# Splitting two key loads of a fused attention and feed-forward kernel into rows 0 to 119 and a shared strip of rows 120 to 127

## The chip, the cores and the metric

The kernel runs on one core of a Trainium2 chip. The metric is the device time of one execution in microseconds, as the median of several runs. A profile of one execution of each kernel is at hand: it tells when each engine's instructions ran, what they waited for, and what the DMA queues moved. The engines are called PE (TensorE), DVE (VectorE), ACT (ScalarE), POOL (GpSimd) and SP (SyncE).

## The reference

Attention over 4 batches, 8 heads, 768 positions and a head size of 64, and behind it a feed-forward layer. Heads 0, 2 and 6 are causal over all keys; the others see a window of 64 positions and the first 4 keys.

```python
scores = scale * np.matmul(q, k.transpose(0, 1, 3, 2))
stream_keep = causal & (is_sink | in_win)
mask = np.where(retr[0, :, 0, 0, None, None], full_mask, stream_mask)
scores = np.where(mask[None, :, :, :], scores, -1000000000.0)
...
a = a / (np.sum(a, axis=-1, keepdims=True) + 1e-09)
return np.matmul(a, v).astype(np.float32)
...
x = np.ascontiguousarray(attn_out.transpose(0, 2, 1, 3)).reshape(B * S, H * D)
h = np.maximum(np.maximum(x @ w1, x @ w2), x @ w3)
return (h @ w_out).astype(np.float32)
```

## The kernel before

The order of all work is written out by hand. `PROGRAM` (lines 84 to 150) is a list of short items; each names a step and its engines, and every engine runs its own instructions in the order in which the items issue them. Nothing is rescheduled.

Batch 0 is loaded differently from the others, since nothing can be computed before it arrives. Its 768 positions are taken in two halves of 384 and its eight heads in four pairs, `PAIRS` = (0,2), (1,3), (4,6), (5,7), counted from 0. `load_pairs` (line 198) brings the keys (`ks`) and the queries (`qs`) of one pair and one half into a staging tile of 128 partitions, three positions to a partition, so that each partition of each head is one run of 768 bytes. These partitions are the "rows" of the title. An item `hl 1 2 2 ss` (line 88) means half 1, from pair 2 on, two pairs, keys and queries both issued by SP: four transfers of 128 rows, two heads and 192 numbers, 192 KB each. `cast_pair` (line 216) turns a staged pair into 16-bit numbers (`kn`, `qn`, line 220), and `turn_pair` (line 228) transposes them on PE into the tile `KQ` that the scores use.

The values of batch 0 come as `vs` (line 298; half 1 is one transfer of 768 KB, item `load_v 0 1 s` in line 91). POOL casts them into `vn` (line 500), PE sorts their rows with `every3` into `vb` (line 508), and ACT and DVE copy these to `va` (line 513).

From batch 1 on, keys and queries come through POOL's queue with a cast on the way (`kq`, line 261, items `load`), four heads at a time, and DVE transposes them into `KQ` (line 275, items `turn`). The scores of these batches are at line 677, their exponentials at line 694, masks at line 380, the product with the values at line 720, and the feed-forward layer at lines 440 (three weights, `w0t`, `w1t`, `w2t`), 448 and 452 (their maximum) and 465 (the output).

SP issues its transfers strictly in order, and so an item `gs 0` (line 286) can hold up what stands behind it: it copies two numbers of a weight into the tile `gates`, which can't be issued before that weight has landed. Each transfer issued by SP or ACT raises one of eight counters, in turn, and before a counter is used again the transfer that used it last has to have landed. A transfer more or less therefore changes which earlier transfer each later one waits for.

Of the kernel before, what the change touches and what calls it, by code (L numbers as in the profile page):

```python
# [12 lines left out]
AF = mybir.ActivationFunctionType  # L13
ALU = mybir.AluOpType

GUESS = (1, 0, 1, 0, 0, 0, 1, 0)
PAIRS = ((0, 2), (1, 3), (4, 6), (5, 7))
ROWS = ((0, 7), (1, 4), (2, 5), (3, 6))
# [135 lines left out]
def fast(ctx, tc, keep, q, k, v, is_retrieval, n_sink, window, moe_w1, moe_w2, moe_w3, moe_w_out, w_t, woutt, out):  # L154
# [4 lines left out]
    P = 128  # L159
# [4 lines left out]
    HALF = S // 2  # L164
    HB = HALF // P
# [4 lines left out]
    assert (H, S, D, DMdl) == (8, 768, 64, 512) and 0 < window <= 64 and 0 <= n_sink <= 64  # L170
    near = [h for h in range(H) if not GUESS[h]]

# [23 lines left out]
    staged, cast, KQs, landed = {}, {}, {}, {}  # L196

    def load_pairs(half, hp, n, engines):
        for nm, src, eng in zip(("ks", "qs"), (k, q), engines):
            st = (  # L200
                pairs2.tile([P, 4, HB, D], FP32, tag=nm, name=nm) if n == 2
                else once.tile([P, 2 * n, HB, D], FP32, name=f"{nm}{hp}")
            )
            for h in range(0, 2 * n, 2):
                h0, h1 = PAIRS[hp + h // 2]
                eng.dma_start(
                    out=st[:, h : h + 2],
                    in_=src[0, h0 : h1 + 1 : h1 - h0, half * HALF : (half + 1) * HALF].rearrange(
                        "h (p j) d -> p h j d", p=P
                    ),  # L210
                )
            for i in range(n):
                staged.setdefault((half, hp + i), []).append(st[:, 2 * i : 2 * i + 2])
                landed[half, hp + i] = st[0:1, 2 * i, 0, 0:2]

    def cast_pair(half, hp, engines):
        cast[half, hp] = []
# [65 lines left out]
    def gate(engine, x):  # L283
        dst = gates[:, next(n_gate)]
        if engine is nc.sync:
            engine.dma_start(out=dst, in_=x)
        else:
            engine.tensor_copy(out=dst, in_=x)
# [21 lines left out]
    def load_first(half, hp, n, e="sc"):  # L310
        by = {"s": nc.sync, "c": nc.scalar}
        load_pairs(half, hp, n, [by[x] for x in e])
# [11 lines left out]
    def idle_work(n):  # L324
# [11 lines left out]
        out=kb[:, 2:4], in_=kb[:, 2:4], compare_op=ALU.is_ge, fill=0.0,  # L336
# [3 lines left out]
        out=kb[:, 3], in_=kb[:, 3], compare_op=ALU.is_gt, fill=0.0,  # L340
# [3 lines left out]
        out=kb[:, 1:5:3], in_=kb[:, 1:5:3], compare_op=ALU.is_gt, fill=0.0,  # L344
# [7 lines left out]
        out=every3, in_=every3, compare_op=ALU.not_equal, fill=1.0,  # L352
# [4 lines left out]
    if n_sink > 0:  # L357
# [4 lines left out]
        out=far, in0=kb[:, 0:5], scalar1=FAR, scalar2=-FAR, op0=ALU.mult, op1=ALU.add  # L362
# [74 lines left out]
    def hidden(b, half, wi, ni, op=None):  # L437
        yy = psum(b, half)
        for ks in range(KS):
            nc.tensor.matmul(  # L440
                yy[:, 0:HALF],
                w_t[wi][:, ks, ni * P : (ni + 1) * P],
                xT[b, half, ks].rearrange("p a t -> p (a t)"),
                start=(ks == 0), stop=(ks == KS - 1),
            )
        if wi == 0:
            acc[b, half, ni] = accp.tile([P, HALF], FP16, tag="acc", name="acc")
            op(out=acc[b, half, ni], in_=yy[:, 0:HALF])  # L448
            return
        if wi == 2:  # L450
            hT[b, half, ni] = htp.tile([P, HALF], FP16, tag=f"hT{ni}", name=f"hT{ni}")
        nc.vector.tensor_tensor(  # L452
            out=acc[b, half, ni] if wi == 1 else hT[b, half, ni],
            in0=yy[:, 0:HALF], in1=acc[b, half, ni], op=ALU.max,
        )
# [59 lines left out]
    def prep_x(b, half, heads, what, op):  # L515
        by_row = b == 0 and half in sorted_halves
        vs = staged_v[b, half] if not by_row else va[0][:, :, half * HB : (half + 1) * HB, 0:D]
        dst = vx[b % 2]
        hs = slice(*map(int, heads.split(":")))
        which = list(range(*hs.indices(H)))  # L520
        xs_ = slice(near.index(which[0]), near.index(which[-1]) + 1)
        n = len(which)
        assert near[xs_] == which
        if what == "r":
            s0 = 2 * half
            k0 = (1, 0)[half]
            op(out=dst[64:P, xs_, s0 : s0 + 2, 0:D], in_=vs[64:P, hs, k0 : k0 + 2])
        else:
            op(  # L529
                out=dst[0:64, xs_, :, 0:D],  # L530
                in_=vs[0:64, hs, 0:1].to_broadcast([64, n, 4, D]),
            )
# [7 lines left out]
    kx = [[consts.tile([P, 4, P, 2], FP16, name=f"kx{j}{quad}") for quad in range(2)] for j in range(2)]  # L540
# [30 lines left out]
    def far_keys(b, quad, op):  # L571
        src, dst = KQs[b, quad][:, 0], kx[b % 2][quad]
        op(
            out=dst[:, :, 64:P].rearrange("p n c two -> p n (c two)"),
            in_=src.rearrange("p (n c) two -> p n (c two)", c=P)[:, 1:5, P : 2 * P],
        )
        if n_sink > 0:
            op(
                out=dst[:, :, 0:n_sink].rearrange("p n c two -> p n (c two)"),
                in_=src[:, 0:n_sink].rearrange("p c two -> p (c two)").unsqueeze(1)  # L580
                .to_broadcast([P, 4, 2 * n_sink]),
            )

    def first_scores(half, u, *hps):
        live = [
            (hp, r, GUESS[PAIRS[hp][r]]) for hp in hps for r in range(2)
            if u < len(FIRST_UNITS[half]["SR"[GUESS[PAIRS[hp][r]]]])
        ]
# [48 lines left out]
    def first_masks(hp, u, r, engine):  # L637
        f = "SR"[GUESS[PAIRS[hp][r % 2]]]
        c, pattern = FIRST_KEEP[f, u]
        mask(pts[0, 1, hp, u], r % 2, 1 if r < 2 else 2, c, P, pattern, engine)  # L640

    def scores(b, s):
        sts, width = {}, {}
        todo = []
        for g in range(G):
            far_row = any(GUESS[h] for h in ROWS[g])
            parts = (MIXED if far_row else NEAR)[s]
# [9 lines left out]
            for r in range(2):  # L657
                for who, kind, ki, q0, n, c0 in parts:
                    quad = (
                        {"T": 0, "S": 1}[who] if not far_row  # L660
                        else [GUESS[h] for h in ROWS[g]].index(who == "R")
                    )
# [139 lines left out]
    def reduce_one(out, in_):  # L802
# [9 lines left out]
        k0=lambda hp, u, r, e: first_masks(int(hp), int(u), int(r), engines[e]),  # L812
        s=lambda b, s: scores(int(b), int(s)),
        k=lambda b, s, xy, i, e: masks(int(b), int(s), xy, int(i), engines[e]),
        f=lambda b, half, wi, ni, *e: hidden(int(b), int(half), int(wi), int(ni), *[ops[x] for x in e]),
# [5 lines left out]
        y=lambda b, half, hs, what, e: prep_x(int(b), int(half), hs, what, ops[e]),  # L821
# [12 lines left out]
        kx=lambda b, quad, e: far_keys(int(b), int(quad), ops[e]),  # L834
# [3 lines left out]
        gs=lambda wi: gate(nc.sync, (w_t + [woutt])[int(wi)][0:1, 0, 0:2]),  # L838
# [206 lines left out]
```

## Time and profile before

| what | us |
|---|---|
| median of 3 runs | 189.18 |
| lowest and highest run | 189.00, 189.24 |
| span of the profiled execution, first to last instruction | 188.2 |
| PE busy in that span | 178.9 |
| DVE busy | 144.1 |
| ACT busy | 99.4 |
| POOL busy | 83.0 |

The profiled execution has no run time of its own; its span is 0.98 us under the median of the runs. The granted clock of PE was 1.000. In the profile an instruction is named by engine, line of the kernel, and the tiles that it writes and reads. "DMA a<-b" in the chain of waits is the time in which the chain waited for that transfer to land. Queue q1 is that of the transfers issued by SP, q10 that of ACT's, q0 that of POOL's.

### The profile page before, as it was taken

What the parts mean: (1) busy time and instruction counts of PE and PEld (TensorE: products, weight loads), DVE (VectorE), ACT (ScalarE), POOL (GpSimd) and SP (SyncE); (2) the same over time, 40 slices, a digit from 0 to 9 for tenths busy, and PEclk for the clock granted to TensorE, in tenths of its full rate; (3) what the DMA queues carried; (4) which work ended last, traced back from release to release, by engine and by line L of the source; (5) the groups of instructions that cost most, each with busy time, mean ns of one, the idle gap of its engine ahead of it and who ended that gap; (6) DMA issues with size and microseconds to landing.
All of it is one profiled execution on the core that took longest, in us unless ns stands there. A gap on an engine that the chain in (4) does not pass through costs nothing.

```text
span 188.2 us, 4755 instructions
## 1 busy us (share of the span) xinstructions
PE 178.9 (95%) x1863; PEld 105.4 (56%) x1863; DVE 144.1 (77%) x306; ACT 99.4 (53%) x161; POOL 83.0 (44%) x142
## 2 busy tenths in 40 slices
PE   7789898999999999999999999999999999999990
PEld 2355546566566456855555556655745574664550
DVE  3749997989899978888979899756874698574540
ACT  3399996368965648687096336764445301311110
POOL 7697899808884890199057002127213400000000
PEclk9999999999999999999999999999999999999999
DMA  5999999998799999439693301321231013301413
GB/s 172 325 329 275 213 212 208 212 229 188 163 130 158 144 280 185 127 74 236 156 262 80 112 0 56 66 80 56 41 87 74 0 62 69 129 0 56 167 56 120
DMA packets 43012, 26.30 MB, mean 140 GB/s; under 512 B 29802, under 2 KB 38506, under 8 KB 42986
## 3 DMA queue, kind: packets, MB, share of 16 engines
q1 hardware_dynamic: 37562, 17.24, 35.6%
q0 software_dynamic: 4192, 7.87, 23.4%
q10 hardware_dynamic: 1232, 0.85, 1.5%
q8 instruction: 15, 0.25, 0.6%
q14 instruction: 11, 0.09, 0.1%
HBM read 25.17 MB, written 6.29 MB: 167 GB/s over the span
## 4 chain that ended last, share of the span: by engine, by line
PE 78%; DMA 13%; DVE 2%; POOL 2%; ACT 2%; issue 1%; ACTq 0%; DVEq 0%; POOLq 0%
PE yy L440 44%; PE yy L465 15%; PE st L677 7%; PE oacc L720 7%; DMA kq<-in_k_dram 7%; DMA qs<-in_q_dram 5%; PE yst L440 3%; DVE KQ L275 2%; DMA ks<-in_k_dram 2%; PE yst L465 1%; DVE acc L452 1%; POOL vx L529 1%; ACT qn L220 0%; ACT pt L632 0%; POOL w1t L401 0%
## 5 line engine op out<-in xcount | busy, mean ns | idle before, releaser
L380 POOL TENSOR_TENSOR pt<-pt,kb 128x512 f16<-128x512 f16 (+5 forms) x53 | 48.3, 931 | 59.7 <-ACT pt L694 51.1
L694 ACT ACTIVATE pt<-st 128x1024 f16<-128x1024 f32 (+2 forms) x51 | 43.5, 908 | 25.1 <-PE st L677 24.7
L440 PE MATMUL yy<-xT,w2t 128*128 128x384 f16 x184 | 36.2, 326 | 0.0
L440 PE MATMUL yy<-xT,w0t 128*128 128x384 f16 x180 | 34.8, 326 | 0.0
L440 PE MATMUL yy<-xT,w1t 128*128 128x384 f16 x176 | 34.3, 326 | 0.0
L465 PE MATMUL yy<-woutt,hT 128*128 128x512 f16 (+1 forms) x138 | 31.4, 372 | 0.0
L452 DVE TENSOR_TENSOR hT<-yy,acc 128x384 f16<-128x384 f32 x46 | 25.2, 555 | 4.6 <-PE yy L440 2.9
L452 DVE TENSOR_TENSOR acc<-yy,acc 128x384 f16<-128x384 f32 x44 | 23.9, 554 | 6.2 <-PE yy L440 4.3
L275 DVE STREAM_TRANSPOSE KQ<-kq 128x384 f32<-128x384 f32 x24 | 25.5, 1131 | 1.3 <-DMA kq<-in_k_dram 1.1
L448 ACT CAST acc<-yy 128x384 f16<-128x384 f32 x27 | 12.9, 492 | 23.5 <-PE yy L440 21.4
L440 PEld LDWEIGHTS <-w0t 128*128 128x128 f16 x192 | 18.1, 98 | 12.8 <-issue 0.7
L440 PEld LDWEIGHTS <-w1t 128*128 128x128 f16 x192 | 17.8, 98 | 12.0 <-issue 0.6
L440 PEld LDWEIGHTS <-w2t 128*128 128x128 f16 x192 | 17.7, 98 | 11.8 <-issue 0.2
L465 PEld LDWEIGHTS <-hT 128*128 128x128 f16 x150 | 14.4, 98 | 15.3
L720 PEld LDWEIGHTS <-pt 128*128 128x128 f16 x472 | 17.2, 97 | 4.2 <-DVE pt L380 0.9
L720 PE MATMUL oacc<-va,pt 128*128 128x65 f16 x392 | 18.6, 193 | 0.8 <-DVE pt L380 0.8
L474 ACT COPY ot<-yy 128x512 f32<-128x512 f32 (+1 forms) x14 | 7.9, 565 | 21.5 <-PE yy L465 18.9
L727 DVE TENSOR_TENSOR x<-oacc,sums 128x384 f16<-128x384 f32 x32 | 17.8, 557 | 1.1
L632 ACT ACTIVATE pt<-st 128x1024 f16<-128x1024 f32 (+5 forms) x22 | 15.4, 769 | 0.4 <-PE st L611 0.2
L677 PE MATMUL st<-KQ 32*128 32x128 f16 (+2 forms) x342 | 15.2, 257 | 0.1
L380 DVE TENSOR_TENSOR pt<-pt,kb 128x256 f16<-128x256 f16 (+4 forms) x31 | 12.4, 405 | 2.1 <-ACT pt L694 2.1
L677 PEld LDWEIGHTS <-KQ 32*128 32x128 f16 x342 | 8.8, 92 | 6.8 <-issue 6.0
(117 smaller groups left out, 190.5 us busy)
## 6 DMA issues: line engine op xcount, KB each, us to landing
out_dram<-ot SPq DMA_DIRECT2D x23, 256.0 KB, 2.0
vs<-in_v_dram SPq DMA_DIRECT2D x18, 256.0 KB, 4.6
ks<-in_k_dram SPq DMA_DIRECT2D x8, 192.0 KB, 3.7
kq<-in_k_dram POOLq DMA_DIRECT2D x3, 384.0 KB, 8.1
kq<-in_q_dram POOLq DMA_DIRECT2D x3, 384.0 KB, 9.6
kq<-in_k_dram POOLq DMA_DIRECT2D x3, 288.0 KB, 5.7
kq<-in_q_dram POOLq DMA_DIRECT2D x3, 288.0 KB, 7.5
qs<-in_q_dram ACTq DMA_DIRECT2D x4, 192.0 KB, 4.9
```

Source lines behind the costliest of these rows:

```text
L275: nc.vector.transpose(out=dst.rearrange("c (p j) -> c j p", j=n)[:, j0:j1], in_=src.rearrange("c (j i) -> c j i", i=R),)
L380: engine.tensor_tensor(out=x, in0=x, in1=of_blocks(kb, pattern, rows), op=ALU.mult)
L440: nc.tensor.matmul(yy[:, 0:HALF], w_t[wi][:, ks, ni * P : (ni + 1) * P], xT[b, half, ks].rearrange("p a t -> p (a t)"), start=(ks == 0), s ...
L448: op(out=acc[b, half, ni], in_=yy[:, 0:HALF])
L452: nc.vector.tensor_tensor(out=acc[b, half, ni] if wi == 1 else hT[b, half, ni], in0=yy[:, 0:HALF], in1=acc[b, half, ni], op=ALU.max,)
L465: nc.tensor.matmul(yo[:, 0:n], hT[b, half, ns][:, tb * P : (tb + 1) * P], woutt[:, ns, c : c + n], start=(ns == 0), stop=(ns == NNB - 1),)
L474: op(out=ot[:, c : c + n], in_=yo[:, 0:n])
L632: nc.scalar.activation(out=pts[0, half, hp, u][:, r0:r1, c0:c1], in_=sts[hp][:, r0:r1, c0:c1], func=AF.Exp, scale=sc,)
L677: nc.tensor.matmul(sts["XY"[g // 2]][:, g % 2, c0 : c0 + n * P], KQ[rows, 0, ki * P : (ki + 1) * P] if kind == "p" else kx[b % 2][quad][ro ...
L694: nc.scalar.activation(out=pts[b, s, xy][:, r0:r1, c0:c1], in_=st[:, r0:r1, c0:c1], func=AF.Exp, scale=sc,)
L720: nc.tensor.matmul(o[:, i, r, 0 : D + 1], at[b, h, kind, ki, qi], vv[:, 0 : D + 1], start=(n == 0), stop=(n == len(todo) - 1), skip_group_ ...
L727: nc.vector.tensor_tensor(out=x, in0=o[:, :, :, 0:D], in1=rc.unsqueeze(3).to_broadcast([P, HB, 2, D]), op=ALU.mult,)
```

## The change

A table `APART` names the loads that are split: half 1, from pair 2 on, keys. For these the staging tile holds the four heads 4, 5, 6, 7 in that order instead of pair by pair. First comes one transfer of rows 120 to 127 of all four heads (8 rows, four heads, 192 numbers, 24 KB), then the two pairs as before, but of rows 0 to 119 only. A pair is then a strided slice of the tile (heads 0 and 2, or 1 and 3 of it). All other loads stay as they are. One of the four items `gs 0` in line 97 goes, so that the number of transfers up to there is the same and the eight counters fall on the same transfers from there on.

```diff
+APART = ((1, 2, "ks"),)
...
-    "y 0 1 4:5:1 r r, gs 0, gs 0, gs 0, gs 0, k0 0 3 2 d, f 0 0 0 5 a, kx 1 0 a, k0 2 1 0 p",
+    "y 0 1 4:5:1 r r, gs 0, gs 0, gs 0, k0 0 3 2 d, f 0 0 0 5 a, kx 1 0 a, k0 2 1 0 p",
...
-            for h in range(0, 2 * n, 2):
-                h0, h1 = PAIRS[hp + h // 2]
+            full, at_pair = P, [slice(2 * i, 2 * i + 2) for i in range(n)]
+            if (half, hp, nm) in APART:
+                full, first = P - 8, PAIRS[hp][0]
+                at_pair = [slice(h0 - first, h1 + 1 - first, h1 - h0) for h0, h1 in PAIRS[hp : hp + n]]
                 eng.dma_start(
-                    out=st[:, h : h + 2],
-                    in_=src[0, h0 : h1 + 1 : h1 - h0, half * HALF : (half + 1) * HALF].rearrange(
-                        "h (p j) d -> p h j d", p=P
+                    out=st[full:P].rearrange("p h j d -> p h (j d)"),
+                    in_=src[0, first : first + 2 * n, half * HALF + full * HB : (half + 1) * HALF].rearrange(
+                        "h (p j) d -> p h (j d)", j=HB
                     ),
                 )
             for i in range(n):
-                staged.setdefault((half, hp + i), []).append(st[:, 2 * i : 2 * i + 2])
-                landed[half, hp + i] = st[0:1, 2 * i, 0, 0:2]
+                h0, h1 = PAIRS[hp + i]
+                eng.dma_start(
+                    out=st[0:full, at_pair[i]],
+                    in_=src[0, h0 : h1 + 1 : h1 - h0, half * HALF : half * HALF + full * HB].rearrange(
+                        "h (p j) d -> p h j d", j=HB
+                    ),
+                )
+            for i in range(n):
+                staged.setdefault((half, hp + i), []).append(st[:, at_pair[i]])
+                landed[half, hp + i] = st[0:1, at_pair[i].start, 0, 0:2]
```

The only engine whose order changes is SP. Here is its order before, from the last query load of half 1's first pairs to the fourth gate on `w0t`; the names in brackets are the counters that an instruction waits for (DMAHW: of SP's and ACT's transfers, DMASW: of POOL's, the others of engines):

```order
L206 DMA qs<-in_q_dram 128x2x192 [waits DMAHW6_49]
L206 DMA ks<-in_k_dram 128x2x192 [waits DMAHW7_49,DVE_49,Pool_49]
L206 DMA ks<-in_k_dram 128x2x192 [waits DMAHW0_49]
L206 DMA qs<-in_q_dram 128x2x192 [waits DMAHW1_49,Activation_49]
L206 DMA qs<-in_q_dram 128x2x192 [waits DMAHW2_49]
L298 DMA vs<-in_v_dram 128x8x192 [waits DMAHW3_49]
L286 DMA gates<-w1t 1x2x1 [waits DMAHW4_49,DMASW3_49]
L286 DMA gates<-w0t 1x2x1 [waits DMAHW5_49,DMASW1_49]
L286 DMA gates<-w0t 1x2x1 [waits DMAHW6_49]
L286 DMA gates<-w0t 1x2x1 [waits DMAHW7_49]
L286 DMA gates<-w0t 1x2x1 [waits DMAHW0_49]
```

The same place on SP after the change (line numbers are 11 higher behind the new code; L209 is the strip):

```order
L217 DMA qs<-in_q_dram 128x2x192 [waits DMAHW6_49]
L209 DMA ks<-in_k_dram 8x4x192 [waits DMAHW7_49,DVE_49,Pool_49]
L217 DMA ks<-in_k_dram 120x2x192 [waits DMAHW0_49]
L217 DMA ks<-in_k_dram 120x2x192 [waits DMAHW1_49]
L217 DMA qs<-in_q_dram 128x2x192 [waits DMAHW2_49,Activation_49]
L217 DMA qs<-in_q_dram 128x2x192 [waits DMAHW3_49]
L309 DMA vs<-in_v_dram 128x8x192 [waits DMAHW4_49]
L297 DMA gates<-w1t 1x2x1 [waits DMAHW5_49,DMASW3_49]
L297 DMA gates<-w0t 1x2x1 [waits DMAHW6_49,DMASW1_49]
L297 DMA gates<-w0t 1x2x1 [waits DMAHW7_49]
L297 DMA gates<-w0t 1x2x1 [waits DMAHW0_49]
```

The strip takes the first key load's place and counter; the two key loads, the two query loads, the values and the first gates each move back by one place and wait for the next counter; three gates on `w0t` are left, and the last of them has the counter that the fourth had. The casts of the two key pairs (DVE and ACT, line 220 before) wait for two counters each, that of the strip and that of their own rows.

## Prediction

> **What bounds the kernel now.** I read the page's busy shares and its 40 slices first, then the chain of waits, then the table by stage, and last the queues and the timeline of the first 40 us. From the page:
>
> ```profile
> PE 178.9 (95%) x1863; PEld 105.4 (56%) x1863; DVE 144.1 (77%) x306; ACT 99.4 (53%) x161; POOL 83.0 (44%) x142
> ...
> PE   7789898999999999999999999999999999999990
> DMA  5999999998799999439693301321231013301413
> ...
> PE 78%; DMA 13%; DVE 2%; POOL 2%; ACT 2%; issue 1%; ACTq 0%; DVEq 0%; POOLq 0%
> ```
>
> The reader should see two stages. For the first seven or eight slices (4.7 us each) the DMA engines are full and PE has holes. After that PE is full to the last slice. The table by stage says the same with a number (time of the stretch, then each engine's busy time; the last column is GB/s):
>
> ```profile
> 12.00:16.00 4.00, 4.00 (x41) 2.06 (x39) 2.81 (x7) 3.81 (x6) 3.31 (x8) 1.00 1.10 326
> ...
> 40.00:60.00 20.00, 19.98 (x256) 12.34 (x258) 18.32 (x37) 14.91 (x22) 13.85 (x28) 1.00 0.91 169
> 60.00:120.00 60.00, 59.98 (x661) 36.00 (x661) 52.69 (x110) 36.06 (x56) 26.86 (x40) 1.00 0.65 139
> ```
>
> From 40 us on PE idles 0.04 us in 80. So the end moves by what PE gains or loses before about 40 us, and by nothing else. The chain of waits in that stretch (start, length, what):
>
> ```profile
> 10.19 4.92 DMA qs<-in_q_dram
> ...
> 19.96 12.38 DMA kq<-in_k_dram
> ...
> 32.46 0.78 DVE KQ L275
> 33.38 0.74 DVE KQ L275
> ...
> 34.34 1.05 DVE acc L452 x2
> 35.39 1.99 DVE KQ L275 x2
> ...
> 37.43 0.61 PE st L677 x10
> 38.04 1.13 PE oacc L720 x33
> ```
>
> Up to 32.34 us it runs through transfers, then through VectorE, and at 37.43 it enters TensorE, which it hardly leaves again.
>
> Two transfers matter. The first is the load of half 1's values (768 KB, the last load of batch 0). Its row gives its size and the time from issue to landing, and below it are the packets of its queue (q1) in 14 to 17, 17 to 22 and 19 to 22 us:
>
> ```profile
> vs<-in_v_dram SPq DMA_DIRECT2D x1, 768.0 KB, 10.5
> ```
>
> ```profile
> q1 hardware_dynamic: 1135, 0.85, 95.4%
> ```
>
> ```profile
> q1 hardware_dynamic: 29, 0.02, 1.8%
> ```
>
> ```profile
> q1 hardware_dynamic: 14, 0.01, 1.5%
> ```
>
> It is issued at 11.53 (row below) and lands 10.5 us later, at 22.0. But the queue moved 1135 packets in the three microseconds up to 17 and then only 29 in five. All but some 0.02 MB of it was there by 17 us; a small share, of one DMA engine or very few, arrives 5 us behind the rest. The second transfer is the key load of batch 1 that lands at 32.34 and runs on the same engines behind it.
>
> Who waits for them, from the timelines of POOL, PE and DVE (the bracket is the idle time before, and what ended it):
>
> ```profile
> 20.48 0.99 POOL L261 DMA_DIRECT2D kq<-in_q_dram  x2
> 22.06 1.59 POOL L500 CAST vn<-vs 128x768 f16<-128x768 f32 x2 [0.59 <-DMA vs<-in_v_dram]
> ```
>
> ```profile
> 23.71 0.59 PE L508 MATMUL vb<-vn,every 128*128 128x512 f16 x2 [0.23 <-POOL vn L500]
> ```
>
> ```profile
> 25.34 0.69 DVE L513 CAST va<-vb 128x512 f16<-128x512 f32 x1 [0.42 <-PE vb L508]
> ```
>
> ```profile
> 29.03 0.20 PE L720 MATMUL oacc<-va,pt 128*128 128x65 f16 x1 [0.82 <-DVE pt L380]
> ```
>
> ```profile
> 32.46 2.08 DVE L275 STREAM_TRANSPOSE KQ<-kq 128x384 f32<-128x384 f32 x2 [1.14 <-DMA kq<-in_k_dram]
> ```
>
> ```profile
> 37.03 1.01 PE L677 MATMUL st<-KQ 32*128 32x384 f16 x18
> ```
>
> **The change part by part.** The sum is made on the profiled execution, whose span is 188.2 us. The median of the runs is 189.18, so 0.98 us lie around the span; I take them as unchanged. A difference under 0.2% (0.38 us) can't be told from none here.
>
> *The late share.* The two key transfers lose staging rows 120 to 127, which is 8 of 128 rows, one sixteenth. The profile counts 16 DMA engines. I assume that a transfer of 128 rows gives each engine eight rows in a row and that one of 120 rows uses fifteen of them, so the engine of the last eight rows is left out of both transfers. No row shows how rows are dealt to engines. The price of a share: 768 KB and 192 KB moved at 326 GB/s (row 12 to 16) give 0.6 us for one 192 KB transfer, in which each engine moves its sixteenth. Two transfers left out give that engine back 1.2 us. If it is the one that trails, everything behind it on that engine comes up to 1.2 us earlier; if it is not, nothing does. That is the unknown of this prediction: bounds 0 and 1.2 us. I take 1.1 us. What I go by is the tail of q1: it is a sliver, not a slow transfer, and the sliver of a row-wise deal most easily left behind is the last one to be handed out.
>
> [...]
>
> *Term 1, the value load.* With the late share 1.1 us earlier, or freed of its tail altogether, the values are there before POOL asks. POOL's own work ends at 20.48 + 0.99 = 21.47, so its casts start 0.59 us earlier, at 21.47. PE then loses the 0.23 us that it waited at 23.71 (it has nothing earlier to do: it gets there at 23.48). DVE's cast of va follows PE and gains the same 0.23 of its 0.42. Its later masks (the wait of 0.82 at 29.03) shift by 0.23 as PE does, so that wait stays as long. Gain 0.23 us; bounds 0 and 0.30, if the hand-over shrinks too.
>
> *Term 2, the key load of batch 1.* DVE waits 1.14 us for it. If the transfer lands at 31.2 instead of 32.34, the four stream transposes end about 1.1 us earlier, near 36.3 instead of 37.38 (35.39 + 1.99). PE starts the group of scores at 37.03 and stalls inside it until 37.43, that is 0.40 us. After term 1 PE is there at 36.80, so the transposes have to be 0.63 us earlier to leave no stall; they have 1.1. Gain 0.40 us; bounds 0 (another engine is next late) and 0.40 (no more is there to gain).
>
> *The strip and the issue slots.* From SP's timeline:
>
> ```profile
> 8.21 1.88 SPq L206 DMA_DIRECT2D ks<-in_k_dram  x2
> 10.19 1.09 SPq L206 DMA_DIRECT2D qs<-in_q_dram  x2
> 11.53 0.37 SPq L298 DMA_DIRECT2D vs<-in_v_dram  x1
> ...
> 31.18 2.36 SPq L286 DMA_DIRECT2D gates<-w0t  x4
> ```
>
> The strip takes the place of the first key issue at 8.21. Everything behind it on SP (two keys, two queries, the values) moves one counter on: the values' issue goes from 11.53 to about 12.1. The queue is full all this time (326 GB/s), the bytes are the same, and the values' transfer starts long after its issue, so I cost this at nothing. If the cover is gone it costs up to the 0.6 us. The waits gain one counter each at the two key casts:
>
> ```profile
> 14.84 0.54 DVE L220 CAST kn<-ks 128x384 f16<-128x384 f32 x1
> 15.83 0.51 POOL L220 CAST qn<-qs 128x384 f16<-128x384 f32 x1 [0.59 <-DMA qs<-in_q_dram]
> 16.88 0.40 POOL L527 COPY vx<-va 64x256 f16<-64x256 f16 x1 [0.54 <-ACT va L513]
> ```
>
> DVE's cast shows no wait for its keys. POOL's query cast does wait, but POOL idles another 0.54 us right behind it, so half a microsecond more or less there is covered. Queued behind them are only these engines' own next steps.
>
> *One gate less.* Four gates take 2.36 us on SP, so the value loads of batch 1 are issued 0.6 us earlier. PE doesn't idle from 40 us on, so nothing waits for them; 0, and I see no loss, since their transfers queue behind what was issued before.
>
> The sum is −0.23 − 0.40 + 0 = −0.63 us: a span of 187.6 and a time of 188.55, say 188.6.
>
> [...]
>
> **The rivals.**
>
> *Nothing (the late share belongs to other rows).* The sliver may be any of sixteen shares; a hold-up that fell on one engine early in the run would look alike. For it: the profile names no engine. Against it: nothing. Then terms 1 and 2 are 0, and so are the rest: 189.2, within 0.1. That the change doesn't do what it says, and 120 rows are dealt out like 128, ends here too.
>
> *Slower (the strip lands on the late engine).* The strip's 32 runs of 768 B have only eight rows to be dealt by, so some engines get four packets more and others none. If the late engine is among them, its tail gets four packets longer. In 19 to 22 us the tail's 14 packets took 3 us, 0.21 each; four make 0.86. The values land at 22.9, POOL and PE's sorting matmuls start 0.86 later, PE reaches the scores at 37.9 instead of 37.03 and the stall of 0.40 there is swallowed: net +0.46, so 189.65. It decides from 0.40 us of delay on; below that the stall hides it. For it: eight of sixteen engines is a large target. Against it: the same packets leave the two big transfers, so the engines of the first 120 rows carry no more than four extra.
>
> *Half the gain.* Another share is next late and comes a few tenths behind: then term 2 shrinks first, term 1 stays, 188.95.
>
> **How the numbers follow.** The forecast gets 0.50, with a range of its own of 188.35 to 188.95 (from the bounds of the two terms; the low end if the wait of 0.82 at 29.03 gives a little as well). Nothing gets 0.28, slower 0.17, half the gain 0.05. For 8 in 10 the range has to take in the first two and part of the slower case: 188.3 to 189.4. Faster by over 0.2%: 0.50 less 0.06 for the part of its own range that is under 0.38 us, 0.44. Within 0.2%: that 0.06, the 0.28 and the 0.05, together 0.39. Slower: 0.17.
>
> **What would show it.** In the profile after, POOL's cast of vn starts near 21.5 with no wait for vs, and the values' transfer lands before that. DVE's transpose starts near 31.4 instead of 32.46. PE's first group of L677 takes 0.6 us instead of 1.01. Term 1 is wrong if POOL still waits for vs; term 2 is wrong if that group still takes 1.0. If q1 still shows a tail of packets after 17 us, the wrong engine was relieved; if that tail is longer and vn starts after 22.5, the slower rival is right. The forecast as a whole is wrong if PE's holes before 40 us add up to what they do now.

## The result and the profile after

The changed kernel takes 190.94 us, median of four runs (190.8, 190.82, 191.07 and 194.67). The kernel before took 189.21 on the same chip. The ratio is 1.0092, with a 95% interval from 1.0068 to 1.0117: slower by 1.7 us, where 0.6 us of gain was forecast. Here and below the ratios leave out runs that are over 1.5% longer than the fastest of the same kernel, like the 194.67, and the profiles of rows_112, cut_96 and one_head_loads are of such runs. The profiled execution of the changed kernel has a span of 188.7 us and a time of 190.8, so 2.1 us lie around the span.

The page of the changed kernel gives the same two stages as before: a full PE behind a first fifth in which DMA is full.

```profile
PE 179.2 (95%) x1863; PEld 106.0 (56%) x1863; DVE 144.4 (77%) x306; ACT 99.7 (53%) x161; POOL 82.9 (44%) x142
...
PE   7989888999999999999999999999999999999990
...
DMA  5999999999789999539794301321222013301413
```

The table by stage of the changed kernel (time of the stretch, the engines' busy times, the clock, the DMA share, GB/s) shows what is new:

```profile
10.00:12.00 2.00, 1.67 (x16) 0.69 (x15) 0.74 (x4) 2.00 (x4) 2.00 (x6) 1.00 1.10 325
12.00:14.00 2.00, 1.67 (x22) 0.93 (x18) 1.05 (x3) 1.91 (x3) 1.22 (x3) 1.00 1.12 216
14.00:16.00 2.00, 2.00 (x19) 0.94 (x16) 1.13 (x3) 1.29 (x4) 1.79 (x3) 1.00 1.07 293
...
12.00:16.00 4.00, 3.67 (x39) 1.87 (x34) 2.18 (x5) 3.19 (x6) 3.01 (x6) 1.00 1.10 255
```

The DMA share stays at 1.1, so the engines are as busy as before, but they move 216 GB/s where they moved 325 just ahead. A 768-byte packet of q1 that starts in these two microseconds takes 59 ns at the median, against 40 in the kernel before. This is the stretch in which the strip and the two loads of 120 rows run. Over 12 to 16 us 255 GB/s stand against 326 before: (326 − 255) × 4 us are 284 KB, which take 0.87 us at 326. The packets of q1 in 14 to 17, 17 to 22 and 19 to 22 us are these:

```profile
q1 hardware_dynamic: 1226, 0.92, 107.8%
```

```profile
q1 hardware_dynamic: 200, 0.14, 11.2%
```

```profile
q1 hardware_dynamic: 77, 0.05, 7.3%
```

The tail behind 17 us, 29 packets before, now has 200. The chain of waits of the changed kernel goes through the load that this tail belongs to (start, length, what):

```profile
11.78 11.05 DMA vs<-in_v_dram
22.88 1.60 POOL vn L511 x2
24.52 1.61 PE vb L519 x9
26.16 0.69 DVE va L524
26.85 1.99 DVE KQ L286 x2
29.85 1.39 PE oacc L731 x39
31.23 1.95 PE yy L451 x12
```

From the values at 22.83 us it runs over POOL's cast, PE's sorting and DVE's copy back into TensorE, on which it stays from 29.85. The timelines of POOL and PE say who waited (start, length, in brackets the idle time before):

```profile
22.88 1.59 POOL L511 CAST vn<-vs 128x768 f16<-128x768 f32 x2 [1.24 <-DMA vs<-in_v_dram]
```

```profile
23.63 0.34 PE L754 MATMUL tr<-ident,x 128*128 128x128 f16 x3
24.52 1.56 PE L519 MATMUL vb<-vn,every 128*128 128x512 f16 x9 [0.55 <-POOL vn L511]
29.85 0.20 PE L731 MATMUL oacc<-va,pt 128*128 128x65 f16 x1 [0.85 <-DVE pt L391]
37.78 0.63 PE L688 MATMUL st<-KQ 32*128 32x384 f16 x18
```

The group of L688 takes 0.63 us, not 1.01: the stall of term 2 is gone. But PE gets there at 37.78 instead of 37.03.

### The profile page after: what moved, and what is told of

It is laid out like the page before. It is cut to its first block, busy times and chain, and to the rows that moved or that the text cites. A ratio compares the mean times of both kernels' runs of the same rounds, so it can differ in the third digit from the quotient of the medians.

```text
span 188.7 us, 4755 instructions
## 1 busy us (share of the span) xinstructions
PE 179.2 (95%) x1863; PEld 106.0 (56%) x1863; DVE 144.4 (77%) x306; ACT 99.7 (53%) x161; POOL 82.9 (44%) x142
## 4 chain that ended last, share of the span: by engine, by line
PE 79%; DMA 14%; DVE 2%; POOL 1%; SPq 0%; issue 0%; ACTq 0%; ACT 0%
PE yy L451 46%; PE yy L476 14%; PE oacc L731 7%; PE st L688 7%; DMA vs<-in_v_dram 6%; DMA xT<-x 3%; PE yst L451 3%; DMA ks<-in_k_dram 3%; DMA qs<-in_q_dram 2%; PE yst L476 1%; DVE KQ L286 1%; PE vb L519 1%; POOL vn L511 1%; PE tr L754 0%; DVE va L524 0%; DVE pt L391 0%
## 5 line engine op out<-in xcount | busy, mean ns | idle before, releaser
L459 ACT CAST acc<-yy 128x384 f16<-128x384 f32 x27 | 12.8, 485 | 23.6 <-PE yy L451 21.5
L731 PEld LDWEIGHTS <-pt 128*128 128x128 f16 x472 | 17.2, 97 | 4.5 <-DVE pt L391 1.0
L688 PE MATMUL st<-KQ 32*128 32x128 f16 (+2 forms) x342 | 14.9, 257 | 0.0
L688 PEld LDWEIGHTS <-KQ 32*128 32x128 f16 x342 | 8.8, 92 | 6.5 <-issue 5.4
```

The lines of the kernel that those rows point to most:

```text
L688: nc.tensor.matmul(sts["XY"[g // 2]][:, g % 2, c0 : c0 + n * P], KQ[rows, 0, ki * P : (ki + 1) * P] if kind == "p" else kx[b % 2][quad][ro ...
L731: nc.tensor.matmul(o[:, i, r, 0 : D + 1], at[b, h, kind, ki, qi], vv[:, 0 : D + 1], start=(n == 0), stop=(n == len(todo) - 1), skip_group_ ...
```

## The experiments

Fourteen runs were made; the median of the kernel before was 189.4 to 189.7 us on the same chips. Two theories were there at the start: S lays the loss to the strip (too small a transfer, or packets on a late engine), U to the two loads that span fewer than 128 rows.

**The kernel before once more** (again_before, no edit).

> The kernel before, unchanged, as a second look at it. Theory A (the late share of the first profile was an accident of that execution): the tail of queue q1 in 17 to 22 us is of another size than 29 packets, and the value load lands at another time than 22.0, while the time stays within 0.3 us of 189.2. Theory B (the same engine always trails): 29 packets again, give or take 5, and a landing within 0.2 us of 22.0. Both expect 326 GB/s in 12 to 16 us and the same time outside the span as in the first profile, about 1.0 us.

Measured: 189.2 us with a span of 187.1, so 2.1 us lie around the span here too. Its stage row, its tail of q1 from 17 to 22 us, and its timelines:

```profile
12.00:16.00 4.00, 4.00 (x42) 2.13 (x41) 3.08 (x7) 3.81 (x7) 3.41 (x9) 1.00 1.10 327
```

```profile
q1 hardware_dynamic: 24, 0.02, 1.2%
```

```profile
21.28 1.60 POOL L500 CAST vn<-vs 128x768 f16<-128x768 f32 x2
```

```profile
22.96 0.34 PE L743 MATMUL tr<-ident,x 128*128 128x128 f16 x3
23.14 1.56 PE L508 MATMUL vb<-vn,every 128*128 128x512 f16 x9
28.24 0.20 PE L720 MATMUL oacc<-va,pt 128*128 128x65 f16 x1 [0.21 <-DVE pt L380]
36.18 0.88 PE L677 MATMUL st<-KQ 32*128 32x384 f16 x18
```

The tail is about as small as in the first profile (24 packets), as theory B had it, but the last of the values lands at 20.44 us instead of 22.0, as theory A had it; both theories missed the 2.1 us. Neither POOL nor PE waits for the values here. The profile from which the forecast was made (span 188.2) was of an execution 1.1 us longer than this one, and the waits of term 1 belonged to that execution. Against this profile the changed kernel is 0.67 us late at PE's transposes (22.96 to 23.63), 1.38 at `vb`, 1.61 at `oacc`, and 1.6 at the end of the span.

**The strip alone** (strip_only): the kernel before with the strip as an extra transfer into a tile that nobody reads then, and one gate fewer.

```diff
+            if (half, hp, nm) == (1, 2, "ks"):
+                spare = woutt.rearrange("p a b -> p (a b)").bitcast(FP32)[P - 8 : P, 0 : 4 * HB * D]
+                eng.dma_start(out=spare..., in_=src[0, 4:8, half * HALF + (P - 8) * HB : (half + 1) * HALF]...)
```

> The kernel before with the strip added (same 8 rows of four heads, into partitions 120 to 127 of a tile that is not in use yet), whole 128-row key loads behind it, and three gates. Theory S (eight engines writing into the same eight partitions hold up all the others): the rate in 12 to 16 us falls from 326 towards the 255 GB/s of the changed kernel, and the time rises by 0.5 us or more. Theory U (it is the 120-row transfers, dealt to fifteen engines, that run slowly): the rate stays over 310 GB/s and the time stays within 0.3 us of before.

Measured: 189.57 us (10 runs), ratio 1.0001 [0.9974, 1.0028].

```profile
12.00:14.00 2.00, 2.00 (x23) 1.14 (x24) 1.07 (x3) 1.90 (x3) 1.94 (x5) 1.00 1.12 297
```

Over 12 to 16 us the rate is 311 GB/s, just over the 310 that U asked for. The strip costs the queue (326 − 297) × 2 us, 58 KB or 0.18 us, and the kernel nothing that can be measured. The extra transfer moves the values' issue to 12.14 us, and neither that nor the missing gate costs anything measurable. S falls.

**The loads of 120 rows without the strip** (no_strip): DVE clears partitions 96 to 127 of the tile instead, so the keys of rows 120 to 127 are left out.

```diff
-                eng.dma_start(out=st[full:P]..., in_=src[...])
+                nc.vector.memset(st[96:P], 0.0)
```

> The changed kernel without the strip: the two key loads of 120 rows alone, four gates as before. Rows 120 to 127 of these keys are zeros instead (a memset of partitions 96 to 127 on DVE ahead of the loads). Theory U: the rate in 12 to 16 us falls nearly as far as in the changed kernel (under 280 GB/s) and the time is over 189.7. Theory S: over 310 GB/s and the time within 0.3 us of before, or below it if the engine that is left out is the late one.

Measured: 199.76 us, ratio 1.0524 [1.0491, 1.0556]. This doesn't tell S from U, for the clearing brought a wait of its own. DVE gets to it late, and SP's key loads stand behind it:

```profile
10.74 0.70 DVE L209 MEMSET ks<- 32x768 f32 x1 [0.22 <-POOL kx L572]
```

```profile
11.46 0.85 SPq L212 DMA_DIRECT2D ks<-in_k_dram  x2
12.41 0.90 SPq L212 DMA_DIRECT2D qs<-in_q_dram  x2
13.35 0.46 SPq L304 DMA_DIRECT2D vs<-in_v_dram  x1
```

All of it is issued 1.6 to 2.1 us later than in the changed kernel (11.46, 12.41 and 13.35 us against 9.36, 10.61 and 11.78), and the values land 17.9 us after their issue. What the run did show is how dear it is when SP falls behind, to which one_head_loads comes back.

**Other cuts** (rows_112, cut_96, cut_64): the changed kernel with 16, 32 or 64 rows in place of 8 in the strip.

```diff
-                full, first = P - 8, PAIRS[hp][0]
+                full, first = P - 16, PAIRS[hp][0]      (P - 32, P - 64)
```

> The changed kernel with the cut at row 112: two key loads of 112 rows and one strip of 16 rows of all four heads. All three divide by 16, so no engine is left out of any. Theory U in the form that the uneven count of engines is what costs: the rate in 12 to 16 us is back over 310 GB/s and the time within 0.3 us of before. Theory U in the form that rows are dealt across the boundaries that 128 rows respect: still under 280 GB/s. Theory S: the strip's 64 runs go to twice as many partitions, so about half of the loss stays.

> The changed kernel with the cut at row 96: rows 96 to 127 of the four heads in one transfer, then rows 0 to 95 of each pair. 'Any cut': at most 265 GB/s in 12 to 16 us and 190.4 to 191.2 us. 'Place': 310 GB/s or more and 189.2 to 189.8 us. If 64 is fast and 96 slow, a cut must be a power of two.

> The changed kernel with the cut at row 64: the four heads' rows 64 to 127 in one transfer, then rows 0 to 63 of each pair. All bytes and gates as in the changed kernel. Theory 'any cut' (a load that spans fewer than 128 rows runs slowly wherever it is cut): at most 265 GB/s in 12 to 16 us and 190.4 to 191.2 us. Theory 'place' (only a cut that is no multiple of 32 rows makes the packets slow): 310 GB/s or more and 189.2 to 189.8 us, the time of the kernel before.

Measured: 190.76 us, ratio 1.004 [1.0011, 1.0069], with 112 rows; 190.42, 1.005 [1.0017, 1.0082], with 96; 191.66, 1.0138 [1.0076, 1.0201], with 64. The stretch of 12 to 14 us with 112, 96 and 64 rows:

```profile
12.00:14.00 2.00, 1.70 (x17) 0.82 (x17) 0.55 (x1) 1.90 (x3) 1.99 (x5) 1.00 1.13 230
```

```profile
12.00:14.00 2.00, 2.00 (x21) 0.98 (x21) 0.82 (x3) 1.90 (x3) 1.42 (x4) 1.00 1.13 227
```

```profile
12.00:14.00 2.00, 1.64 (x19) 0.85 (x17) 0.82 (x3) 1.91 (x3) 1.61 (x5) 1.00 1.14 199
```

Every cut is slow; the 191.66 us with 64 rows are even above the 190.4 to 191.2 expected. That one engine has nothing to do with 120 rows is not the reason, since each load of these three runs leaves sixteen landing marks in the trace (times at which a part of it was reported as landed, read here as one for each engine); nor does a cut at a multiple of 32 help, as the theory "place" had it.

**Half the dose and twice the dose** (one_pair_cut, both_cut): only pair 2's keys cut, with its heads side by side as before; and the queries of both pairs cut as well.

```diff
+                cut = (half, hp, nm, h) == (1, 2, "ks", 0)
+                for a, b in ((P - 8, P), (0, P - 8)) if cut else ((0, P),):
...
-APART = ((1, 2, "ks"),)
+APART = ((1, 2, "ks"), (1, 2, "qs"))
```

> The kernel before with pair 2's keys alone cut at row 120 (rows 120 to 127 of its two heads in one transfer, then rows 0 to 119), the heads side by side in the tile as before. One transfer more and one gate fewer, as in the changed kernel. 'Cut': about half of the changed kernel's loss of rate, 280 to 305 GB/s in 12 to 16 us, and 189.7 to 190.5 us. 'Apart': 315 GB/s or more and 189.2 to 189.8 us.

> The changed kernel with the queries of the same two pairs cut at row 120 as well, one gate fewer for the one transfer more: twice the dose. If the loss is the slow packets of the cut loads, it doubles: the rate in 12 to 16 us falls to some 200 to 220 GB/s, the values land 0.8 us or more later than in the changed kernel, and the time is 191.8 to 192.8 us. If the loss is a single slip behind one wait, the time stays at 190.6 to 191.3 us.

Measured: 190.35 us, ratio 1.0033 [1.0001, 1.0065], with one pair; 195.55, ratio 1.0308 [1.0242, 1.0375], with both keys and queries. The stretch of 12 to 16 us with one pair:

```profile
12.00:16.00 4.00, 4.00 (x43) 2.19 (x40) 2.89 (x6) 3.71 (x7) 3.04 (x6) 1.00 1.11 290
```

Half the dose loses half the rate (326 − 290 = 36, against 71 GB/s) and about half the time. With twice the dose the rate is 223 GB/s, just above the 200 to 220 expected, so the loss (103) is less than doubled; but the time lost is 6 us, not 2.4 to 3.4. POOL's timeline shows where:

```profile
26.96 1.60 POOL L511 CAST vn<-vs 128x768 f16<-128x768 f32 x2 [4.78 <-DMA vs<-in_v_dram]
```

It waits 4.78 us for the values. Something else joins in, which one_head_loads shows. And behind the wait PE is slower: the granted clock (one digit to each 4.86 us) falls in 24.3 to 34.0 us, and the group `vb` takes 2.84 us where it takes 1.56 in the changed kernel.

```profile
PEclk9999985999999999999999999999999999999999
```

```profile
28.61 2.84 PE L519 MATMUL vb<-vn,every 128*128 128x512 f16 x9 [4.28 <-POOL vn L511]
```

**The order of heads alone, and one transfer for all four** (strided, one_load): the kernel before with the four heads in order in the tile, loaded as two pairs of 128 rows; and with all four in one transfer of 128 rows.

```diff
+                at_pair = [slice(h0 - first, h1 + 1 - first, h1 - h0) for h0, h1 in PAIRS[hp : hp + n]]
...
+                eng.dma_start(out=st, in_=src[0, first : first + 2 * n, half * HALF : (half + 1) * HALF]...)
```

> The kernel before with one thing of the change alone: the four heads of the two key pairs stand in order in the tile, so that a pair's load of all 128 rows writes heads two places apart. Nothing is cut, and the number of transfers is that of the kernel before. Theory 'apart' (writing heads that do not adjoin is what slows the packets): at most 265 GB/s in 12 to 16 us and 190.2 to 191.2 us. Theory 'cut' (fewer rows than 128 in a load is what slows them): 320 to 330 GB/s and 189.2 to 189.8 us.

> The kernel before with the keys of both pairs in one transfer of 128 rows of all four heads, one gate more for the one transfer fewer. Nothing is cut. If cutting the rows is what costs, the rate stays at 320 to 330 GB/s and the time at 189.2 to 189.8 us (0.6 us of issue are saved on a queue that is full anyway). If the order of the rows in the tile (all heads together) is what costs, the rate falls below 290 GB/s and the time is above 190.2 us.

Measured: 189.77 us, ratio 1.0009 [0.9986, 1.0033], and 189.14 us, ratio 1.0 [0.9978, 1.0022]. The stretch of 12 to 14 us of strided is that of the kernel before:

```profile
12.00:14.00 2.00, 2.00 (x24) 1.13 (x24) 1.08 (x3) 1.90 (x3) 1.99 (x6) 1.00 1.10 327
```

So the strided tile, the other new thing about these loads, costs nothing measurable, and a load of 128 rows may have four heads. One transfer fewer gains nothing that can be measured either; no version beat the kernel before.

**As few pieces, but all rows** (one_head_loads): the kernel before with the keys of the two pairs in four transfers of one head and 128 rows.

```diff
+                heads = [(h, h0), (h + 1, h1)] if (half, hp, nm) == (1, 2, "ks") else [(h, None)]
```

> The kernel before with the keys of the two pairs in four transfers of one head and all 128 rows each (two transfers more, two gates fewer). A transfer then has 128 pieces of 768 bytes, just as many as a load of 64 rows of two heads, which ran at 178 to 230 GB/s. Theory 'rows' (fewer than 128 rows in a load slow it): 320 to 330 GB/s in 12 to 14 us, 189.2 to 190.2 us. Theory 'small' (fewer than 256 pieces in a load slow it): at most 260 GB/s in 12 to 14 us and over 190.4 us.

Measured: 328 GB/s in 12 to 14 us, and still 195.41 us (four runs from 191.12 to 197.53, too far apart for a ratio). The rate speaks for "rows"; the time is neither's. The loads of 64 rows in cut_64 had run at 199 GB/s in 12 to 14 us and 230 in 12 to 16. The rows of one_head_loads: the stage, then SP's and POOL's issues, then both queues' packets from 15 to 16 us, then POOL's wait.

```profile
12.00:14.00 2.00, 2.00 (x24) 1.01 (x20) 1.36 (x3) 1.90 (x3) 1.99 (x4) 1.00 1.11 328
```

```profile
12.26 0.37 SPq L302 DMA_DIRECT2D vs<-in_v_dram  x1
```

```profile
11.86 0.75 POOL L265 DMA_DIRECT2D kq<-in_k_dram  x1
```

```profile
q0 software_dynamic: 57, 0.18, 88.2%
q1 hardware_dynamic: 56, 0.04, 17.8%
```

```profile
27.48 1.59 POOL L504 CAST vn<-vs 128x768 f16<-128x768 f32 x2 [6.70 <-DMA vs<-in_v_dram]
```

Two transfers more on SP push the values' issue to 12.26 us, behind POOL's first key load of batch 1 at 11.86. In 15 to 16 us the two queues go packet by packet: 57 of q0 and 56 of q1, but those of q0 are some four times as large (0.18 against 0.04 MB), so SP's queue gets a fifth of the bytes. The values land 15 us after their issue. In all profiles the order of these two issues goes with the first packets of q0 (time of the values' issue less that of the key load; q0's packets in 14 to 16 us). The profiles left out of the table have the values ahead and no packets.

| kernel | us | packets |
|---|---|---|
| again_before | −0.77 | 0 |
| changed kernel, and again | −0.19, −0.09 | 0, 0 |
| rows_112, cut_96 | +0.14, +0.19 | 2, 6 |
| one_head_loads, both_cut | +0.40, +0.45 | 109, 47 |
| no_strip, kq_before_vs | +0.97, +1.11 | 53, 102 |

**The order of the two issues by itself** (kq_before_vs, after_kq_late): in the kernel before, POOL's key load moved ahead of its value casts; in the changed kernel, moved behind two of its key and query casts.

```diff
-s0 0 0 3, vc 0 0 4 p, ... turnp 1 0 dd, load 1 0 0, cast 1 1 pp
+s0 0 0 3, load 1 0 0, vc 0 0 4 p, ... turnp 1 0 dd, cast 1 1 pp
...
-turnp 1 0 dd, load 1 0 0, cast 1 1 pp
+turnp 1 0 dd, cast 1 1 pp, load 1 0 0
```

> The kernel before with GpSimd's first key load of batch 1 issued ahead of its two casts of values, at 10.4 us in place of 12.4, and so ahead of SyncE's value load at 11.6 us. Nothing is cut. Theory 'order' (the value load goes at full rate only where SyncE issues it before GpSimd's key load; else the two share the engines packet by packet): the first packets of GpSimd's queue run by 14.5 us, the values land after 23 us and the time is over 191.5 us. Rival (the order of issue does not matter, GpSimd's packets come as their descriptors are ready): its packets start 2 us earlier, the values land by 22.5 us and the time is 189.0 to 190.3 us.

> The changed kernel with GpSimd's first key load of batch 1 put behind its two casts of key and query pairs, at some 14.5 us in place of 12.0, so that it is surely behind SyncE's value load. 'Order': the slow executions (values behind the key load) go, while the cut's own 0.9 us stays: 190.2 to 191.0 us, with GpSimd's first packets at 16.8 to 17.3 us as in the changed kernel. Rival (GpSimd's packets start a fixed 4 to 5 us after its issue): they start after 18 us, the values land by 18.5 us, and the time is 189.2 to 189.9 us.

Measured: 190.79 us, ratio 1.0044 [1.0006, 1.0082], for the first; 190.54 us, ratio 1.0066 [1.0026, 1.0106], for the second. The order does matter, but less than expected here: the key load's packets ran from 13.1 us on, the last of SP's query loads landed at 17.18 us (15.80 in again_before), and POOL came to its cast at 22.50 without a wait for values, PE to `vb` at 24.33. The values landed at 22.45, within the rival's bound of 22.5 and not behind 23, as 'order' expected. In the second, q0's packets began at 17.2 us though issued 2.9 us later, so their start is no fixed time behind the issue: they came as SP's queue ran out (1189 packets of q1 in 14 to 17 us, 262 in 17 to 22). No packet of q1 is left there after 19 us, and POOL doesn't wait for the values:

```profile
22.14 1.60 POOL L511 CAST vn<-vs 128x768 f16<-128x768 f32 x2
```

```profile
24.32 1.57 PE L519 MATMUL vb<-vn,every 128*128 128x512 f16 x9
```

And yet `vb` is only 0.20 us earlier than in the changed kernel: PE itself comes to it 1.18 us later than in again_before (24.32 against 23.14) with no wait for values, and its span is 0.9 us longer (188.0 against 187.1). The late values are one way in which the cut's lost time reaches PE, not the only one. The long executions were expected to go and did not: 192.43 and 192.6 us are among the ten runs.

**The changed kernel once more** (after_again, no edit).

> The changed kernel once more, unchanged, for a second profile and more times. If the cut's cost is a property of its loads and not of one execution: 245 to 265 GB/s in 12 to 16 us and 190.4 to 191.1 us. If the first profile of it was an accident, as that of the kernel before partly was: over 290 GB/s and 189.4 to 190.0 us.

Measured: 190.67 us, ratio 1.007 [1.0026, 1.0113], span 188.6. The profile repeats the first:

```profile
12.00:16.00 4.00, 4.00 (x42) 2.12 (x41) 1.94 (x4) 3.49 (x5) 3.11 (x6) 1.00 1.09 250
```

```profile
23.06 1.60 POOL L511 CAST vn<-vs 128x768 f16<-128x768 f32 x2 [1.13 <-DMA vs<-in_v_dram]
```

```profile
24.70 1.56 PE L519 MATMUL vb<-vn,every 128*128 128x512 f16 x9 [0.46 <-POOL vn L511]
```

The profiled executions whose time is known, put together, tie the time to the start of that group `vb` of half 1:

| kernel | `vb` starts, us | time of that execution, us |
|---|---|---|
| one_load, again_before, strided, strip_only | 22.48, 23.14, 23.27, 23.46 | 189.39, 189.2, 189.18, 189.13 |
| after_kq_late, kq_before_vs, changed kernel, again | 24.32, 24.33, 24.52, 24.70 | 190.0, 190.18, 190.8, 190.62 |
| cut_64, both_cut, no_strip | 25.34, 28.61, 32.99 | 191.33, 196.31, 199.96 |
| long runs: cut_96, rows_112, one_head_loads | 25.94, 26.93, 29.12 | 192.85, 193.4, 196.25 |

Up to 23.5 us nothing depends on it; behind that the time rises by more than the delay. From strip_only to cut_64 it is 2.2 us for 1.9, and to both_cut 7.2 for 5.2, where the lower clock shown above is part of it. one_pair_cut is off this line, 189.90 at 23.13.

## Why the prediction was wrong

**What bounds the kernel.** That PE is full from 40 us on and that the end moves by what happens before held: the 1.61 us at `oacc` are the 1.6 at the end.

**The execution that was read.** "I take them as unchanged" of the 0.98 us around the span was the first slip. In the profiled executions whose time is known, 1.7 to 2.2 us lie around the span (189.13 less 187.4 in strip_only, 189.39 less 187.2 in one_load; 2.1 in again_before and in the changed kernel). By that the first profile was of an execution of about 190 us, not of 189.2. Both terms of the sum were taken from it. In again_before the waits of term 1 don't exist at all, and the stall of term 2 is 0.25 us (0.88 less 0.63) instead of 0.40. There was next to nothing to gain.

**The late share.** The assumption was that one engine has rows 120 to 127, and that it is the one that trails. The trace bears out the number of engines, if a landing mark stands for one: each load of 120 rows leaves fifteen landing marks, the strip eight, a load of 128 rows sixteen. It also fits that one engine was relieved: the first mark of the two query loads behind the cut loads comes 0.73 and 0.72 us ahead of the second (13.96 and 14.69, 14.60 and 15.32), in again_before 0.08 and 0.08; that is less than the 1.1 us taken. That the relieved engine is the late one failed: the tail after 17 us grew from 29 packets to 200, and it is no longer one share. In the first profile fifteen of the values' sixteen marks come by 18.74 us and one at 22.01; in the changed kernel twelve come behind 18.4, the last at 22.83. Eight rows in a row to an engine, and that the last share is the one most easily left behind, were the author's own assumptions. No run here shows which engine wrote which rows.

**Terms 1 and 2.** −0.23 became a wait of POOL for the values of 1.24 us where a usual execution has none, and `vb` came 1.38 us later. The stall of term 2 did go, but as the slower rival had it: PE came later and found its keys there.

**The strip and the issue slots, the step that failed.** "The queue is full all this time (326 GB/s), the bytes are the same, … so I cost this at nothing." The bytes were the same and the queue was full, but 326 GB/s was a property of loads of 128 rows and not of the queue. Loads cut at 120, 112, 96 and 64 rows ran with their strips at 216 (229 in after_again), 230, 227 and 199 GB/s in 12 to 14 us, uncut ones of 96, 192 and 384 KB at 326 to 328. The 0.87 us so lost make the two key loads land at 14.62 and 15.29 us instead of 14.00 and 14.61 in again_before (PE is 0.67 us late by 23.6 us) and stretch the values' tail into the time in which POOL's queue runs (200 packets of q1 beside 505 of q0 in 17 to 22 us). The strip alone is 0.18 us of it. Why fewer rows are slower no run shows.

**The issue of the values** was put at 12.1 us and was 11.78; by itself the slot costs nothing measurable (strip_only, 12.14). What the step left out is POOL's key load, issued at 11.97: the values' lead over it is 0.19 us. Where the lead was lost, the two queues shared the engines, and one_head_loads took 195.41 us; but one of its four runs took 191.12, and kq_before_vs, which lost the lead by more, 190.79. The order alone doesn't settle how much is lost.

**One gate less** costs nothing measurable: strip_only has it too.

**The slower rival** named the right path (values at 22.9, then POOL and PE; 22.83 was measured) with a wrong cause and about a quarter of the size, 0.46 us net. Its price was measured against an execution in which 1.1 us had already been lost. It is also the rival that the prediction's own signs point to: a longer tail, and `vn` behind 22.5 us (22.88).

**What stays open.** Why the cut loads are slow, beyond the number of rows; how much of the 1.7 us goes through the keys and how much through the values; why some runs of the changed kernel and of its kin are 2 to 4 us longer. A lost lead of the values over POOL's key load (0.45 us behind it in both_cut), with a lower clock of PE behind the wait (0.50 there), could do that by the author's estimate, but no profile of such an execution of the changed kernel was taken.

## What to carry to other kernels

The rate that the queue showed belonged to the shapes that ran in it, 326 to 328 GB/s with whole loads and 199 to 230 with cut ones: before a load is cut along the partitions, ask what rate the cut shape has, not only whether the bytes stay the same. Add up span and time over several executions before a wait of half a microsecond is taken for the kernel's own, for one profile can be 1 us off (here a span of 188.2 us against 187.1). And where one queue's large transfer is to run before another's, see how far apart their issues are, since one more transfer in front can turn the order (the values 0.77 us ahead in again_before, 0.14 behind in rows_112).

## What the runs showed of the hardware that was not expected

Loads of fewer than 128 partitions ran with their strips at 199 to 230 GB/s in this kernel (12 to 14 us with 120, 112, 96 and 64 rows) while the DMA engines count as fully busy (a share of 1.12 to 1.14, against 1.10 in again_before), and whole loads behind them are back at over 320 (331 GB/s in 15 to 16 us of the changed kernel). In two stretches in which both queues had work they shared the engines packet by packet (57 against 56 in 15 to 16 us of one_head_loads, 61 against 62 in 14 to 15 us of kq_before_vs), although the packets of one were some four times as large (0.18 against 0.04 MB in the first). POOL's packets, issued at 12.0 or at 14.8 us, began at 17.1 and 17.2, as SP's ran out (1226 and 1189 packets of q1 in 14 to 17 us, 200 and 262 in 17 to 22). And behind a wait of 4.28 us PE ran at half its clock (0.50 in 28 to 34 us of both_cut), while behind one of 0.55 us in the changed kernel it stayed at 1.00.
